# Attention plus gated feed-forward on one core: the first three blocks of chunk 0 spread over the attention rounds, another order of loads, useless matmuls in the first waits

## Chip, cores, metric

One core of one Trainium2 chip. The metric is device time in microseconds (us) of one execution. "Faster" and "slower" in a verdict mean by more than 2%.

## The reference, cut to what matters

```python
# q, k, v: (8 batches, 8 heads, 576 positions, 64), float32
kv  = np.einsum('bhsd,bhse->bhde', k, v)
out = np.einsum('bhsd,bhde->bhse', q, kv)
rms = np.sqrt(np.mean(out * out, axis=-1, keepdims=True) + 1e-06)
x   = out / rms * g_norm                       # heads side by side: (4608, 512)
gate = 1.0 / (1.0 + np.exp(-(x @ w_gate)))     # weights (512, 1536), float64
return (gate * (x @ w_val)) @ w_out            # (1536, 512), float64
```

The weights come as float64, so the kernel converts them from bits on VectorE and ScalarE.

## The kernel before

It works on pairs of heads. A pair goes through these steps; the letters are used throughout:

```python
# K   K'V (12 matmuls) and the q transposes (6)        TensorE
# KVO copy of K'V to SBUF          VectorE  | QO  copy of transposed q   ScalarE
# U   q times K'V (5 matmuls)      TensorE  | SQ  square                 ScalarE
# SUM row sums                     VectorE  | ROOT square root           ScalarE
# NORM reciprocal, scaling         VectorE  | X   transposes (5)         TensorE
# XO  scale by g_norm into xT      ScalarE
```

xT of chunk 0 (512 tokens) is made from pairs 0 to 3 (batch 0). Pairs 4 to 7 (batch 1) are needed for chunk 1. The first layer of chunk 0 has twelve blocks f of 8 matmuls (4 of the gate, 4 of the value, 128x512 each); block f needs weights unit f, converted in five VectorE steps and two ScalarE steps:

```python
def s0():
    ...                                             # m = mantissa bits            VectorE
    vec.tensor_scalar(out=m.bitcast(U32), in0=words(u)[1], scalar1=0x000FFFFF, ...)
    nc.scalar.activation(out=m, in_=m.bitcast(U32), func=AF.Identity, scale=2.0 ** -20, bias=one)
def s1():                                           # p = exponent                 VectorE, ScalarE
    ...
def s2(): ...                                       # low word added               VectorE
def s3(): ...                                       # sign                         VectorE
def s4():
    vec.tensor_tensor(out=m, in0=m, in1=d["p"].bitcast(FP32), op=ALU.mult)
    load_unit(u + NST)
...
for n in range(4):
    load_kv(n)
    load_q(n)
    if n == 0:
        load_unit(0)
```

The start of the kernel is in the order of a list of tokens. `c` is one conversion step, `w1` the load of unit 1, `b013` block 0, value, part 3 of 4:

```python
order = """
    K0 QO0 KVO0 U0 c c SQ0 c SUM0 K1 c ROOT0 NORM0 X0 QO1 KVO1 w1 c U1 XO0 K2 SQ1 SUM1 b000 KVO2
    ROOT1 QO2 NORM1 b010 U2 X1 SQ2 K3 XO1 SUM2 ROOT2 b001 KVO3 QO3 w2 NORM2 U3 X2 SQ3 K4 XO2 SUM3
    ...
    SUM5 ROOT5 b012 KVO6 QO6 NORM5 U6 c X5 SQ6 K7 XO5 SUM6 ROOT6 b003 KVO7 QO7 NORM6 U7 c X6 SQ7
    b013 XO6 SUM7 b100 c ROOT7 b110 G NORM7 b101 E X7 c b111 XO7 c b102 b112 c b103 c b113
"""
```

So each round of attention holds one matmul of block 0; of block 1 three matmuls come ahead of the last X, and the rest of it, with blocks 2, 3 and on, comes after the rounds. Later stages (second layer of chunk 0, chunks 1 to 8) aren't touched.

Of the kernel before, what the change touches and what calls it, by code (L numbers as in the profile page):

```python
# [9 lines left out]
FP32 = mybir.dt.float32  # L10
# [3 lines left out]
AF = mybir.ActivationFunctionType  # L14
ALU = mybir.AluOpType
# [4 lines left out]
def kernel(  # L20
# [11 lines left out]
    nc = tc.nc  # L32

    B, H, S, HD = q.shape
    T, DM = out.shape
    DF = moe_w_gate.shape[1]
    P = 128
# [7 lines left out]
    M = S // NU  # L45
# [4 lines left out]
    NFT = DF // P  # L50
    G = 512
    GH = G // 2
    NG = T // G
    NST = 3
# [12 lines left out]
    NE = 2 * NHP  # L67
# [5 lines left out]
    def load_kv(n):  # L73
        if n >= B * NHP:
            return
        b, h0 = n // NHP, 2 * (n % NHP)
        for name, src in (("k", k), ("v", v)):
            t = (first if n < NE else sb).tile([NP, 2, NJ * HD], FP32, tag=name, name=name, bufs=4 if n < NE else 2)
            nc.sync.dma_start(out=t, in_=src[b, h0:h0 + 2].rearrange("h (p j) d -> p h (j d)", j=NJ))
            pairs[n][name] = t  # L80
# [12 lines left out]
    units = [("gv", f) for f in range(NFT)] + [("wo", f) for f in range(0, NFT, 2)]  # L93
# [4 lines left out]
    def load_unit(u):  # L98
        if u >= len(units):
            return  # L100
        kind, f = units[u]
        staged[u] = st = raw.tile([P, 2, DM], I64, tag="st", name="st", bufs=NST)
        for i in range(2):
            if kind == "gv":
                src = (moe_w_gate, moe_w_val)[i].rearrange("(m p) f -> p m f", p=P)[:, :, P * f:P * f + P]
                nc.sync.dma_start(out=st[:, i].rearrange("p (m f) -> p m f", m=NMT), in_=src)
            else:
                nc.sync.dma_start(out=st[:, i], in_=moe_w_out[P * (f + i):P * (f + i) + P, :])

    def words(u):  # L110
        t = staged[u].rearrange("p i f -> p (i f)").bitcast(U32).rearrange("p (n two) -> p n two", two=2)
        return t[:, :, 0], t[:, :, 1]
# [8 lines left out]
    def convert(u):  # L121
        kind, f = units[u]
        vec = nc.vector
        d = {}

        def s0():

            t = const.tile([P, 2, DM], FP32, name=f"{kind}{f}") if kind == "gv" else w2[:, f:f + 2, :]
            if kind == "gv":
                for i, name in enumerate(("wg", "wv")):  # L130
                    w[name, f] = t[:, i].rearrange("p (m f) -> p m f", m=NMT)
            else:
                for i in range(2):
                    w["wo", f + i] = t[:, i]
            d["m"] = m = t.rearrange("p i f -> p (i f)")
            vec.tensor_scalar(out=m.bitcast(U32), in0=words(u)[1], scalar1=0x000FFFFF, scalar2=None,
                              op0=ALU.bitwise_and)
            nc.scalar.activation(out=m, in_=m.bitcast(U32), func=AF.Identity, scale=2.0 ** -20, bias=one)

        def s1():  # L140


            d["p"] = p = raw.tile([P, UW], U32, tag="cz", name="cz", bufs=2)
            vec.tensor_scalar(out=p, in0=words(u)[1], scalar1=20, scalar2=0x7FF, op0=ALU.logical_shift_right,
                              op1=ALU.bitwise_and)
            nc.scalar.activation(out=p.bitcast(I32), in_=p, func=AF.Relu, scale=2.0 ** 23, bias=exp_off)

        def s2():

            m = d["m"]  # L150
            vec.scalar_tensor_tensor(out=m, in0=words(u)[0], scalar=2.0 ** -52, in1=m, op0=ALU.mult, op1=ALU.add)

        def s3():
            p = d["p"]
            vec.scalar_tensor_tensor(out=p, in0=words(u)[1], scalar=0x80000000, in1=p, op0=ALU.bitwise_and,
                                     op1=ALU.bitwise_or)

        def s4():
            m = d["m"]
            vec.tensor_tensor(out=m, in0=m, in1=d["p"].bitcast(FP32), op=ALU.mult)  # L160
            load_unit(u + NST)

        return [s0, s1, s2, s3, s4]

    STEPS = 5
    converts = deque(step for u in range(len(units)) for step in convert(u))
    made = [0]

    def convert_some(n):
        for _ in range(min(n, len(converts))):  # L170
            converts.popleft()()
            made[0] += 1

    def converted(u):
        convert_some(STEPS * (u + 1) - made[0])

    for n in range(4):
        load_kv(n)
        load_q(n)
        if n == 0:  # L180
            load_unit(0)


    w2 = const.tile([P, NFT, DM], FP32, name="w2")
    ident = const.tile([P, P], FP32, name="ident")
# [138 lines left out]
    def gv_tile(c, f):  # L324
        gv[c, f] = hp.tile([P, G], FP32, tag="gv", name="gv")
        return gv[c, f]

    def sg_tile():
        return sb.tile([P, G], FP32, tag="sg", name="sg", bufs=4)
# [14 lines left out]
    psum_ctx = tc.tile_pool(name="psum0", bufs=1, space=bass.MemoryType.PSUM)  # L344
    psum0 = psum_ctx.__enter__()

    def at_ps(kind):
        return psum_at.tile([P, 2, 512], FP32, tag="at", name="at")
# [15 lines left out]
    def mm_ps():  # L364
        return psum.tile([P, 512], FP32, tag="mm", name="mm", bufs=6)
# [19 lines left out]
    late = deque()  # L385

    def plain(c, f, ps):

        converted(f)
        blk = Plain(c, f, ps)  # L390
        for at in range(2 * NMT):
            blk.mm(*divmod(at, NMT))
            if at in (0, 2) and late:
                late.popleft()()
            if at < STEPS:
                convert_some(1)
        late.extend([blk.gate, blk.end])


    KV, KV_OUT, Q, Q_OUT, U, U_SQUARE, U_SUM, U_ROOT, U_NORM, X, X_OUT = range(11)  # L400
    a = [attention(n, early(n)) for n in range(NE)]

    steps = {"K": (KV, Q), "KVO": (KV_OUT,), "QO": (Q_OUT,), "U": (U,), "SQ": (U_SQUARE,), "SUM": (U_SUM,),
             "ROOT": (U_ROOT,), "NORM": (U_NORM,), "X": (X,), "XO": (X_OUT,)}

    order = """
        K0 QO0 KVO0 U0 c c SQ0 c SUM0 K1 c ROOT0 NORM0 X0 QO1 KVO1 w1 c U1 XO0 K2 SQ1 SUM1 b000 KVO2
        ROOT1 QO2 NORM1 b010 U2 X1 SQ2 K3 XO1 SUM2 ROOT2 b001 KVO3 QO3 w2 NORM2 U3 X2 SQ3 K4 XO2 SUM3
        ROOT3 b011 KVO4 QO4 NORM3 U4 c X3 SQ4 K5 XO3 SUM4 c ROOT4 b002 KVO5 QO5 NORM4 U5 c X4 SQ5 K6 XO4
        SUM5 ROOT5 b012 KVO6 QO6 NORM5 U6 c X5 SQ6 K7 XO5 SUM6 ROOT6 b003 KVO7 QO7 NORM6 U7 c X6 SQ7  # L410
        b013 XO6 SUM7 b100 c ROOT7 b110 G NORM7 b101 E X7 c b111 XO7 c b102 b112 c b103 c b113
    """
    blks = {}

    def block01(f):
        if f not in blks:
            t = psum0.tile([P, 2, 512], FP32, tag="kq", name="two") if f else at_ps(None)
            blks[f] = Plain(0, f, [t[:, i] for i in range(2)])
        return blks[f]

    for token in order.split():
        name = token.rstrip("0123456789")
        n = token[len(name):]
        if name == "b":
            block01(int(n[0])).mm(int(n[1]), int(n[2]))
        elif name == "c":
            convert_some(1)
        elif name == "w":
            load_unit(int(n))
        elif name == "G":  # L430
            blks[0].gate()
        elif name == "E":
            blks[0].end()
        else:
            for step in steps[name]:
                a[int(n)][step]()
            if token == "K7":
                first_ctx.__exit__(None, None, None)
                hp = ctx.enter_context(tc.tile_pool(name="hp", bufs=21))
    late.extend([blks[1].gate, blks[1].end])  # L440
    at0 = at_ps(None)
    plain(0, 2, [at0[:, i] for i in range(2)])
    psum_ctx.__exit__(None, None, None)
    psum = ctx.enter_context(tc.tile_pool(name="psum", bufs=1, space=bass.MemoryType.PSUM))
    for f in range(3, NFT):
        plain(0, f, (mm_ps(), mm_ps()))

    ps = [mm_ps() for _ in range(G // P)]
# [3 lines left out]
                         skip_group_check=True)  # L452

    for f in range(0, NFT - 2, 2):
        converted(NFT + f // 2)
        for at in range(2 * G // P):
            second(at % (G // P), f + at // (G // P))
            if late:
                late.popleft()()
            if at < STEPS:  # L460
                convert_some(1)
    raw_ctx.__exit__(None, None, None)


# [12 lines left out]
    sx, tw, s12, s4 = {}, {}, {}, {}  # L477
# [205 lines left out]
```

## Time and profile before

| | before |
|---|---|
| time, median of 4 runs | 1122.92 us (1121.94 to 1125.1) |
| span of the profiled run | 1120.8 us |
| TensorE busy | 1099.2 us (98%) |
| first matmul of chunk 0 | 23.06 us |
| first matmul of block 3 | 68.64 us |

"Busy" of TensorE counts matmuls with modelled ends, so 98% doesn't say that it can't be faster. Two marks are used below to compare runs, both from TensorE's instructions in order of time: the start of chunk 0's first matmul, and the start of block 3. From block 3 to the end of the span it is 1052.2 us in the trace before. A float32 matmul shows as two records in the profile, its halves, so x4 of block 0 are two matmuls. The lines themselves are in the prediction.

### The profile page before, as it was taken

The page shows a single profiled execution, that of the slowest core. Times are in us where ns is not written, and L with a number is a line of the kernel's source. Part 1 is how long each engine was busy: PE and PEld are TensorE (multiplying, and loading weights), DVE is VectorE, ACT ScalarE, POOL GpSimd, SP SyncE. Part 2 cuts the span into 40 slices and gives each one's busy share as a digit, 9 for nine tenths or more (in the row PEclk, how much of TensorE's full clock was granted, in tenths as well). Part 3 has the DMA queues.
Part 4 walks back from the last instruction along what each step waited for, and adds up shares of the span by engine and source line. Part 5 has one row for each costly group of instructions (what it writes and reads, how often), then busy time and mean ns, then how long its engine had stood idle before and what let it go on. Part 6 is the DMA issues. An engine that isn't in the chain of part 4 may idle for free.

```text
span 1120.8 us, 15097 instructions
## 1 busy us (share of the span) xinstructions
PE 1099.2 (98%) x5760; PEld 912.4 (81%) x5760; DVE 570.6 (51%) x1155; ACT 317.8 (28%) x613; POOL 279.3 (25%) x390
## 2 busy tenths in 40 slices
PE   6899999999999999999999999999999999999998
PEld 5544447888888888888888888888888888888887
DVE  3687776554255516552455326551556146615541
ACT  3643321332133303340333214330333022101110
POOL 0000023432043203330243114320333044404420
PEclk9999999999999999999999999999999999999999
DMA  9944412021202012200302120202100000010001
GB/s 231 264 150 151 150 37 80 22 54 30 72 12 54 11 42 54 53 20 19 73 11 54 30 72 11 54 12 61 41 12 1 20 19 1 1 29 10 1 1 38
DMA packets 71591, 57.60 MB, mean 51 GB/s; under 512 B 40800, under 2 KB 65376, under 8 KB 71520
## 3 DMA queue, kind: packets, MB, share of 16 engines
q1 hardware_dynamic: 71360, 56.64, 19.1%
q8 instruction: 46, 0.75, 0.3%
q14 instruction: 25, 0.20, 0.1%
q10 hardware_dynamic: 160, 0.00, 0.0%
HBM read 47.19 MB, written 9.44 MB: 51 GB/s over the span
## 4 chain that ended last, share of the span: by engine, by line
PE 95%; DVE 2%; ACT 1%; issue 1%; DMA 1%; SPq 0%; ACTq 0%; DVEq 0%
PE mm L510 51%; PE mm L590 26%; PE mm L375 6%; PE mm L451 4%; PE at L246 2%; PE at L217 2%; PE at L231 1%; PE at L272 1%; PE at L375 1%; PE two L246 1%; DMA st<-in_moe_w_val_dram 1%; PE two L217 0%; PE two L375 0%; PE two L272 0%; DVE gv L546 0%
## 5 line engine op out<-in xcount | busy, mean ns | idle before, releaser
L496 POOL TENSOR_TENSOR tw<-gv 128x256 f32<-128x256 f32 x192 | 140.0, 740 | 790.7 <-PE mm L510 628.1
L510 PE MATMUL mm<-xT,tw 128*128 128x256 f32 x768 | 182.4, 380 | 1.0 <-DVE gv L522 1.0
L510 PE MATMUL mm<-sx,tw 128*128 128x256 f32 x768 | 182.4, 380 | 0.0
L510 PE MATMUL mm<-xT,gv 128*128 128x256 f32 x768 | 181.6, 379 | 0.0
L510 PEld LDWEIGHTS mm<-xT,gv 128*128 128x128 f32 x768 | 145.5, 190 | 20.1 <-issue 0.5
L510 PEld LDWEIGHTS mm<-xT,tw 128*128 128x128 f32 x768 | 143.3, 190 | 20.2 <-issue 1.8
L510 PEld LDWEIGHTS mm<-sx,tw 128*128 128x128 f32 x768 | 144.1, 190 | 19.0
L496 POOL TENSOR_TENSOR tw<-gv,tw 128x256 f32<-128x256 f32 x192 | 144.5, 773 | 0.0
L539 ACT ACTIVATE sg<-sg 128x256 f32<-128x256 f32 x96 | 39.9, 417 | 213.1 <-DVE sg L538 213.1
L530 DVE TENSOR_TENSOR gv<-mm,sg 128x256 f32<-128x256 f32 x96 | 40.8, 425 | 99.5 <-PE mm L510 99.5
L510 PE MATMUL mm<-sx,gv 128*128 128x256 f32 x384 | 90.9, 379 | 0.0
L590 PE MATMUL mm<-t2w,gv 128*128 128x256 f32 x384 | 89.0, 379 | 0.0
L590 PE MATMUL mm<-w,gv 128*128 128x256 f32 x384 | 88.3, 379 | 0.0
L590 PE MATMUL mm<-w,s 128*128 128x256 f32 x384 | 88.1, 379 | 0.0
L590 PEld LDWEIGHTS mm<-w,s 128*128 128x128 f32 x384 | 72.9, 190 | 9.9
L590 PEld LDWEIGHTS mm<-t2w,gv 128*128 128x128 f32 x384 | 72.5, 190 | 9.6
L590 PEld LDWEIGHTS mm<-w,gv 128*128 128x128 f32 x384 | 72.4, 190 | 9.6
L510 PEld LDWEIGHTS mm<-sx,gv 128*128 128x128 f32 x384 | 72.1, 190 | 9.4
L517 ACT COPY sg<-mm 128x256 f32<-128x256 f32 x96 | 35.8, 373 | 154.1 <-PE mm L510 154.1
L546 DVE TENSOR_TENSOR gv<-gv,sg 128x512 f32<-128x512 f32 x96 | 78.7, 860 | 0.2
L543 DVE TENSOR_TENSOR gv<-mm,gv 128x256 f32<-128x256 f32 x96 | 40.7, 424 | 47.9 <-PE mm L510 47.5
L526 ACT ACTIVATE sg<-mm 128x256 f32<-128x256 f32 x96 | 36.3, 384 | 100.8 <-PE mm L510 100.8
(94 smaller groups left out, 1130.3 us busy)
## 6 DMA issues: line engine op xcount, KB each, us to landing
k<-in_k_dram SPq DMA_DIRECT2D x32, 288.0 KB, 4.8
v<-in_v_dram SPq DMA_DIRECT2D x32, 288.0 KB, 5.1
q<-in_q_dram SPq DMA_DIRECT2D x64, 144.0 KB, 3.0
st<-in_moe_w_gate_dram SPq DMA_DIRECT2D x12, 512.0 KB, 3.7
st<-in_moe_w_val_dram SPq DMA_DIRECT2D x12, 512.0 KB, 4.9
st<-in_moe_w_out_dram SPq DMA_DIRECT2D x12, 512.0 KB, 4.0
out_dram<-sg SPq DMA_DIRECT2D x24, 192.0 KB, 2.3
out_dram<-sg SPq DMA_DIRECT2D x24, 128.0 KB, 2.3
```

What stands on the lines that cost most here:

```text
L246: nc.tensor.matmul(d["u"][:, i], qT[:, M * i:M * i + MU], kvs[n % 2], start=True, stop=True)
L375: nc.tensor.matmul(self.ps[i], w[("wg", "wv")[i], self.f][:, m, :], xT[self.c][:, m, :], start=(m == 0), stop=(m == NMT - 1), skip_group_c ...
L451: nc.tensor.matmul(ps[t], gv[0, f][:, P * t:P * t + P], w["wo", f], start=(f == 0), stop=(f == NFT - 1), skip_group_check=True)
L496: nc.gpsimd.tensor_tensor(out=tw[f, i], in0=b[in0], in1=b[in1] if isinstance(in1, tuple) else tw[f, in1], op=ALU.subtract)
L510: nc.tensor.matmul(ps, wt[:, m, :], xs[:, m, :], start=(new and m == 0), stop=(m == NK - 1), skip_group_check=True)
L517: nc.scalar.copy(out=d["sg"][:, h2], in_=pa)
L526: nc.scalar.activation(out=d["sg"][:, h1], in_=pa, func=AF.Sigmoid)
L530: tt(out=d["h"][:, h2], in0=pb, in1=d["sg"][:, h2], op=ALU.add)
L539: nc.scalar.activation(out=d["sg"][:, h2], in_=d["sg"][:, h2], func=AF.Sigmoid)
L543: tt(out=d["h"][:, h1], in0=pc, in1=d["h"][:, h1], op=ALU.add)
L546: tt(out=d["h"], in0=d["h"], in1=d["sg"], op=ALU.mult)
L590: nc.tensor.matmul(ps, hs(f), ws[:, f, :], start=(new and f == 0), stop=(f == NF2 - 1), skip_group_check=True)
```

## The change

Intent: TensorE waits in the first 60 us and hardly later, so give it chunk 0's blocks as filling there; load in the order in which data is wanted; keep TensorE busy while it waits, so that it runs fast. Its core:

```diff
-        if n == 0:
+        if n == 1:
             load_unit(0)
...
-    order = """
-        K0 QO0 KVO0 U0 c c SQ0 c SUM0 K1 c ROOT0 ...
+    order = """
+        warm10 KV0 Q0 KVO0 QO0 w1 warm3 U0 SQ0 KV1 SUM0 ROOT0 Q1 KVO1 NORM0 QO1 warm3 U1 SQ1 SUM1 X0 c0.0 c0.1
+        XO0 ROOT1 NORM1 warm5 KV2 Q2 KVO2 a0.0 c0.2 X1 a0.1 c0.3 c0.4 QO2 w2 warm2 U2 SQ2 KV3 Q3 b0.0.0 b0.1.0
+        KVO3 XO1 QO3 w3 U3 SUM2 KV4 Q4 ROOT2 NORM2 SQ3 SUM3 ROOT3 X2 XO2 b0.0.1 b0.1.1 b0.0.2 NORM3 X3 KVO4 QO4
+        U4 c1.0 a1.0 c1.1 a1.1 c1.2 c1.3 b0.1.2 KV5 Q5 KVO5 XO3 b0.0.3 b0.1.3 SQ4 c1.4 w4 SUM4 QO5 U5 CG0 CV0
+        KV6 Q6 b1.0.0 ROOT4 NORM4 X4 b1.1.0 b1.0.1 b1.1.1 SQ5 SUM5 ROOT5 KVO6 QO6 XO4 U6 NORM5 X5 c2.0 c2.1 a2.0
+        c2.2 b1.0.2 KV7 Q7 SQ6 SUM6 a2.1 b1.1.2 ROOT6 c2.3 b1.0.3 XO5 b1.1.3 KVO7 QO7 U7 c2.4 NORM6 CG1 X6 CV1
+        b2.0.0 SQ7 XO6 b2.1.0 b2.0.1 c3.0 SUM7 ROOT7 b2.1.1 c3.1 a3.0 a3.1 NORM7 X7 XO7 c3.2 c3.3 c3.4 b2.0.2
+        b2.1.2 b2.0.3 c4.0 S0 S1 b2.1.3 M0 G2 M1 b3.0.0 b3.1.0 a4.0 E2 c4.1 a4.1 c4.2 c4.3 b3.0.1 b3.1.1 b3.0.2
+        b3.1.2 b3.0.3 b3.1.3 c4.4
     """
...
+        elif name == "CG":                     # gate of the block leaves PSUM as it is
+            copies[f, 0] = sg_tile()
+            nc.scalar.copy(out=copies[f, 0], in_=blks[f].ps[0])
+        elif name == "CV":
+            copies[f, 1] = sg_tile()
+            nc.vector.tensor_copy(out=copies[f, 1], in_=blks[f].ps[1])
+        elif name == "S":                      # sigmoid later, on SBUF
+            nc.scalar.activation(out=copies[f, 0], in_=copies[f, 0], func=AF.Sigmoid)
+        elif name == "M":
+            nc.vector.tensor_tensor(out=gv_tile(0, f), in0=copies[f, 1], in1=copies[f, 0], op=ALU.mult)
+        elif name == "warm":
+            for _ in range(f):
+                nc.tensor.matmul(two0[:, 0, 0:P], ident, ident, start=True, stop=True)
```

Here `c0.2` is step 2 of unit 0 on VectorE, `a0.1` the ScalarE part of a step, `b0.1.3` block 0, value, part 3. K is split in KV and Q. `warm10` is ten useless matmuls: the identity times itself, a result that nobody reads. The blocks of the rounds share one pair of tiles (gate, value) of PSUM, the memory in which matmuls leave their sums; `CG` and `CV` copy a finished block out of it, so that the next can have it.

More of the change, by code (lines that the diff above doesn't have):

```diff
@@ L137, in s0, with a0 @@
                               op0=ALU.bitwise_and)
+        def a0():
+            m = d["m"]
             nc.scalar.activation(out=m, in_=m.bitcast(U32), func=AF.Identity, scale=2.0 ** -20, bias=one)
@@ L145, in s1, with a1 @@
                               op1=ALU.bitwise_and)
+        def a1():
+            p = d["p"]
             nc.scalar.activation(out=p.bitcast(I32), in_=p, func=AF.Relu, scale=2.0 ** 23, bias=exp_off)
@@ L160, in s4, with convert_step @@
             vec.tensor_tensor(out=m, in0=m, in1=d["p"].bitcast(FP32), op=ALU.mult)
-            load_unit(u + NST)
-        return [s0, s1, s2, s3, s4]
-    STEPS = 5
-    converts = deque(step for u in range(len(units)) for step in convert(u))
-    made = [0]
-    def convert_some(n):
-        for _ in range(min(n, len(converts))):
-            converts.popleft()()
-            made[0] += 1
-    def converted(u):
-        convert_some(STEPS * (u + 1) - made[0])
+            if u > 1:
+                load_unit(u + NST)
+        return {"c": [s0, s1, s2, s3, s4], "a": [a0, a1]}
+    conversion = [convert(u) for u in range(len(units))]
+    def convert_step(u, i):
+        if u < len(units) and i < 5:
+            conversion[u]["c"][i]()
+            if i < 2:
+                conversion[u]["a"][i]()
     for n in range(4):
@@ L387, in plain @@
     def plain(c, f, ps):
-        converted(f)
         blk = Plain(c, f, ps)
@@ L394, in plain @@
                 late.popleft()()
-            if at < STEPS:
-                convert_some(1)
+            convert_step(f + 1, at)
         late.extend([blk.gate, blk.end])
@@ L401 @@
     a = [attention(n, early(n)) for n in range(NE)]
-    steps = {"K": (KV, Q), "KVO": (KV_OUT,), "QO": (Q_OUT,), "U": (U,), "SQ": (U_SQUARE,), "SUM": (U_SUM,),
-             "ROOT": (U_ROOT,), "NORM": (U_NORM,), "X": (X,), "XO": (X_OUT,)}
+    steps = {"KV": KV, "KVO": KV_OUT, "Q": Q, "QO": Q_OUT, "U": U, "SQ": U_SQUARE, "SUM": U_SUM, "ROOT": U_ROOT,
+             "NORM": U_NORM, "X": X, "XO": X_OUT}
     order = """
-        K0 QO0 KVO0 U0 c c SQ0 c SUM0 K1 c ROOT0 NORM0 X0 QO1 KVO1 w1 c U1 XO0 K2 SQ1 SUM1 b000 KVO2
-        ROOT1 QO2 NORM1 b010 U2 X1 SQ2 K3 XO1 SUM2 ROOT2 b001 KVO3 QO3 w2 NORM2 U3 X2 SQ3 K4 XO2 SUM3
-        ROOT3 b011 KVO4 QO4 NORM3 U4 c X3 SQ4 K5 XO3 SUM4 c ROOT4 b002 KVO5 QO5 NORM4 U5 c X4 SQ5 K6 XO4
-        SUM5 ROOT5 b012 KVO6 QO6 NORM5 U6 c X5 SQ6 K7 XO5 SUM6 ROOT6 b003 KVO7 QO7 NORM6 U7 c X6 SQ7
-        b013 XO6 SUM7 b100 c ROOT7 b110 G NORM7 b101 E X7 c b111 XO7 c b102 b112 c b103 c b113
@@ L412 @@
-    """
-    blks = {}
-    def block01(f):
-        if f not in blks:
-            t = psum0.tile([P, 2, 512], FP32, tag="kq", name="two") if f else at_ps(None)
-            blks[f] = Plain(0, f, [t[:, i] for i in range(2)])
-        return blks[f]
+        warm10 KV0 Q0 KVO0 QO0 w1 warm3 U0 SQ0 KV1 SUM0 ROOT0 Q1 KVO1 NORM0 QO1 warm3 U1 SQ1 SUM1 X0 c0.0 c0.1
+        XO0 ROOT1 NORM1 warm5 KV2 Q2 KVO2 a0.0 c0.2 X1 a0.1 c0.3 c0.4 QO2 w2 warm2 U2 SQ2 KV3 Q3 b0.0.0 b0.1.0
+        KVO3 XO1 QO3 w3 U3 SUM2 KV4 Q4 ROOT2 NORM2 SQ3 SUM3 ROOT3 X2 XO2 b0.0.1 b0.1.1 b0.0.2 NORM3 X3 KVO4 QO4
@@ L421 @@
+        b3.1.2 b3.0.3 b3.1.3 c4.4
+    """
+    blks, copies = {}, {}
+    two0 = at_ps(None)
     for token in order.split():
-        name = token.rstrip("0123456789")
-        n = token[len(name):]
+        name = token.rstrip("0123456789.")
+        n = [int(i) for i in token[len(name):].split(".")]
+        f = n[0]
         if name == "b":
-            block01(int(n[0])).mm(int(n[1]), int(n[2]))
-        elif name == "c":
-            convert_some(1)
-        elif name == "w":
-            load_unit(int(n))
-        elif name == "G":
-            blks[0].gate()
-        elif name == "E":
-            blks[0].end()
-        else:
-            for step in steps[name]:
-                a[int(n)][step]()
-            if token == "K7":
+            if f not in blks:
+                if f == 3:
+                    psum_ctx.__exit__(None, None, None)
+                    psum = ctx.enter_context(tc.tile_pool(name="psum", bufs=1, space=bass.MemoryType.PSUM))
+                    ps = (mm_ps(), mm_ps())
+                else:
+                    t = at_ps(None) if f else two0
+                    ps = (t[:, 0], t[:, 1])
+                blks[f] = Plain(0, f, ps)
+            blks[f].mm(n[1], n[2])
+        elif name == "CG":
[8 more added lines that the diff above has]
+            nc.vector.tensor_tensor(out=gv_tile(0, f), in0=copies[f, 1], in1=copies[f, 0], op=ALU.mult)
+        elif name == "G":
+            blks[f].gate()
+        elif name == "E":
+            blks[f].end()
+        elif name in ("c", "a"):
+            conversion[f][name][n[1]]()
+        elif name == "w":
+            load_unit(f)
+        elif name == "warm":
+            for _ in range(f):
+                nc.tensor.matmul(two0[:, 0, 0:P], ident, ident, start=True, stop=True)
+        else:
+            a[f][steps[name]]()
+            if token == f"Q{NE - 1}":
@@ L438 @@
                 first_ctx.__exit__(None, None, None)
                 hp = ctx.enter_context(tc.tile_pool(name="hp", bufs=21))
-    late.extend([blks[1].gate, blks[1].end])
-    at0 = at_ps(None)
-    plain(0, 2, [at0[:, i] for i in range(2)])
-    psum_ctx.__exit__(None, None, None)
-    psum = ctx.enter_context(tc.tile_pool(name="psum", bufs=1, space=bass.MemoryType.PSUM))
-    for f in range(3, NFT):
+    late.extend([blks[3].gate, blks[3].end])
+    for f in range(4, NFT):
         plain(0, f, (mm_ps(), mm_ps()))
@@ L454 @@
     for f in range(0, NFT - 2, 2):
-        converted(NFT + f // 2)
         for at in range(2 * G // P):
@@ L459 @@
                 late.popleft()()
-            if at < STEPS:
-                convert_some(1)
+            convert_step(NFT + 1 + f // 2, at)
     raw_ctx.__exit__(None, None, None)
```

## The prediction

> **What bounds the kernel now.** I read the busy table by stretches first, then the list of what TensorE waited for, then TensorE's instructions in order of time, then the other engines and the transfers over the same stretch. The busy table (length, then TensorE, weight loads, VectorE, ScalarE, GpSimd, then granted clock, DMA share, GB/s):
>
> ```profile
> 0.00:20.00 20.00, 9.69 (x79) 8.63 (x80) 7.86 (x17) 6.40 (x10) 0.70 (x6) 1.00 1.01 229
> 20.00:40.00 20.00, 17.39 (x183) 12.98 (x181) 9.73 (x22) 11.73 (x25) 0.00 (x0) 1.00 1.08 267
> 40.00:60.00 20.00, 17.80 (x131) 11.57 (x132) 14.42 (x22) 12.03 (x25) 0.00 (x0) 1.00 0.82 197
> 60.00:80.00 20.00, 19.23 (x46) 8.38 (x45) 17.82 (x21) 8.84 (x10) 0.00 (x0) 1.00 0.49 159
> 80.00:100.00 20.00, 20.00 (x48) 8.77 (x47) 15.58 (x18) 7.96 (x9) 0.00 (x0) 1.00 0.47 156
> 160.00:1121.00 961.00, 955.13 (x5140) 835.46 (x5138) 455.92 (x1006) 248.28 (x514) 276.19 (x382) 1.00 0.12 31
> ```
>
> From 80 us on TensorE is full, and in the last 961 us it idles 5.9 us, most of that the tail. The idle time lies in the first 60 us, where the change works: 15.1 us there. No other engine is full there, but the DMA share is about 1 until 54 us. The list of TensorE's waits in the first 62 us (in total, times, longest):
>
> ```profile
> PE two L217 <- DMA v<-in_v_dram: 7.0, 2, 5.2
> PE two L246 <- ACT qT L236: 3.5, 5, 1.9
> PE two L272 <- DVE sq L263: 3.2, 2, 1.9
> PE two L246 <- DVE kv L223: 1.3, 1, 1.3
> PE at L375 <- ACT sg L380: 0.8, 1, 0.8
> ```
>
> And TensorE in order of time (start, length, what):
>
> ```profile
> 5.17 1.55 PE L217 MATMUL two<-v,k 96*64 96x64 f32 x24 [5.17 <-DMA v<-in_v_dram]
> 6.65 1.22 PE L231 MATMUL two<-ident,q 96*128 96x96 f32 x6
> 9.18 2.45 PE L246 MATMUL two<-kv,qT 128*116 128x128 f32 x10 [1.31 <-DVE kv L223]
> ...
> 18.21 1.19 PE L272 MATMUL two<-ident,sq 115*128 115x115 f32 x5 [1.85 <-DVE sq L263]
> 19.20 2.34 PE L246 MATMUL two<-kv,qT 128*116 128x128 f32 x10
> ...
> 23.06 1.91 PE L375 MATMUL at<-xT,gv 128*128 128x512 f32 x4
> ...
> 49.34 1.35 PE L246 MATMUL two<-kv,qT 128*116 128x128 f32 x10 [0.41 <-ACT qT L236]
> ```
>
> The same ten instructions take 2.45 us at 9 us and 1.35 us at 49 us: TensorE is slow until about 21.5 us. In the middle each attention round (4.65 us, from one U group to the next) holds only one matmul of chunk 0, so TensorE waits 0.41 us for the q copy in most rounds, and 1.85 us where a weight conversion stands ahead of it. Blocks 1, 2 and 3 come after the rounds, all but alone on TensorE.
>
> **What the work alone would take.** Groups back to back and fast, from their distances in the chain that ended last: K'V 0.85, Q transposes 0.66, U 1.09, X transposes 0.49 us: 3.09 a pair, 24.7 us for eight pairs. A matmul of chunk 0 is 0.858 us (the chain has 144 half-matmuls, so 72 matmuls, in 61.80 us), a block of eight 6.87, four blocks 27.5. Together 52.2 us. Block 2 ends in the chain at 68.81 us, so block 3 at 75.7. The first real matmul can't start before v lands at 5.1 us. So 75.7 - 5.2 - 52.2 = 18.3 us are lost; 10.6 are the waits above (without the first 5.2), some 5.4 the slow matmuls, the rest ends of groups. **18 us, 1.6% of the span, is all that the change can win**; 2% would be 22.5.
>
> **What the Trainium skill says.** "TensorE: Matmul & The Clock Gate", Part 1: the array runs at half its clock until about 3.4 us of sustained activity, and falls back after an idle window of that length. The trace agrees in the durations (1.55 against 0.92 us for K'V; busy without a gap from 18.21, fast from about 21.5, 3.3 us later), but its granted clock says 1.00 throughout and doesn't show it. "DMA: Bandwidth & Descriptors", "Issuing engines are not separate DMA queues": transfers share the same 16 engines, so an order of loads moves landings but adds no bandwidth; here 11.3 MB had landed at 47.4 us, some 250 GB/s after the start. "ScalarE: Activation LUTs", "What ACT_TABLE_LOAD costs": some 1.28 us a load; the trace shows 1.28 us at 54.64, between the root of the last pair and the first sigmoid. "Perfetto Trace Analysis", "Optimization Strategy": interleave regimes with different limits; that is what this change does.
>
> **The change part by part.**
>
> *Useless matmuls.* 23 of 128 columns, two halves each. A half is 0.213 us slow and 0.109 fast (ten of U in 2.13 and 1.09 us). The first ten start when the identity is written (1.3 us) and take about 4.3 us, to 5.6: 0.4 us past v's landing, which costs about that; but K'V and Q then run fast, which wins 1.2 us in the first two groups and 1.1 in U0. The other 13 (some 2.8 us) lie in gaps of the chains of pairs 0 to 2.
>
> *Another order of loads.* Unit 0 of the weights now follows pair 1, not pair 0. By bytes, at the times by which before had moved as much: pair 1 by 10.2 us instead of 14.2, unit 0 by 14.2 instead of 11.5, pair 2 by 18, pair 3 by 22 (as before), unit 1 by 29.5, pair 7 by 43, unit 3 by 47.3.
>
> *Where conversions stand.* The changed kernel, built, has the same arithmetic; added are two copies on each of ScalarE and VectorE (about 0.6 us each), by which blocks 0 and 1 leave PSUM with no sigmoid, so that no table load falls among the roots, and the one PSUM pair is free for the next block. Two sigmoids on SBUF follow (1.0 us). One conversion of a unit is 0.6 + 0.6 + 3 x 1.15 = 4.7 us of VectorE and 2.2 of ScalarE.
>
> *The first 24 us*, followed by hand through the new order on all engines with the durations above: K'V0 5.6, q copy to 8.5, U0 to 9.9, its norm to 13.0, U1 12.7 to 14.0, unit 0's first two steps on VectorE 15.6 to 16.8, norm 1 to 18.0, K'V2 from 17.2 (data), unit 0's last three steps 18.6 to 22.1 (before: to 19.7), Q3 at 22.0 (data), first two matmuls of chunk 0 22.7 to 24.4. By then TensorE has done 4 K'V, 4 Q, 3 U, 2 X and 2 matmuls: 6.0 + 3.3 + 1.0 + 1.7 = 12.0 us. Before, these same started at 23.06, so the start itself wins little.
>
> *From 24.4 on* 40.2 us of TensorE work are left to the end of block 3: 64.6 us if it waits no more. Does the rest keep up? VectorE from 22.1 to the end of unit 3's conversion: 5 kv copies 2.3, 6 norms of 1.86 11.2, three units 14.1, two copies 1.3: 28.9 us. In program order, with its waits for ScalarE and for the landings, I get unit 1 at 35.1 (block 1 starts at 38.4), unit 2 at 48.3 (block 2 at 50.5), unit 3 at 57.0 (block 3 at 57.8). ScalarE has about 24 us in that stretch. PSUM: the copies of block 1 end at 50.0, half a us before block 2 wants it. Unit 4 must be converted for 64.7; the table load and sigmoids come first on ScalarE (55.5 to 58.4), and I get 63.2. All close, none late: block 3 ends at 64.7.
>
> *The sum.* 75.7 - 64.7 = 11.0 us. Everything after is the same work, with TensorE full (a block asks 4.7 + 0.7 us of VectorE in 6.9), so nothing gives it back. I take off 1 us, as hand chains leave out handovers and margins are under 1 us in four places: 10.3 us, **1113.0 us**.
>
> **The rivals.** *VectorE becomes the bound.* It is asked 28.9 us in 35, in a strict order where every norm waits for a square and a root. The 1.9 us wait at 40 us before, behind one conversion step, speaks for it. If the margins fail by 2 or 3 us in all, the gain is 7 to 8: 1115 to 1117. *The transfers bound the start.* Pair 2 and pair 3 wait for data in my chain as well, and the DMA share is 1. If the rate there is a tenth lower, everything up to unit 3 lands 2 to 4 us later: gain 7 to 9. For the change: the order puts no weight before it is wanted. *TensorE stays or falls slow.* The gaps between groups up to 17 us may keep the clock down in spite of the useless matmuls; then U0 to U2 and K'V cost about 3 us more on the chain: gain 8, 1115. *The end was hidden anyway*: a later wait (weights, output) eats it: nothing speaks for it, the stretch from 80 us on has full TensorE and half-busy DMA; it would give 1121. *Better than by hand*: first data sooner, or conversion ready at 20 us: 13 to 14, 1109 to 1110.
>
> **Range and chances.** The rivals together lie at 1109 to 1118, which is the range: 1109.0 to 1118.0. More than 2% faster is barred by the 18 us: 0.01. Within 2%: 0.98. Slower by 2%: 0.01, only if the later part is disturbed.
>
> **What would show it right or wrong.** Right: K'V of pair 0 in about 0.9 us at 5.6; the first matmul of chunk 0 at 22 to 23 us; TensorE over 19 us busy of each 20 after 25 us; block 3 done at about 65 us; one table load at about 56 us. Wrong by VectorE: TensorE's waits list shows norm or converted weights (gv) with over 3 us. Wrong by the transfers: K'V or the conversions waiting on DMA after 15 us. Wrong by the clock: U groups of over 2 us after 8 us. And if block 3 is done at 65 but the span is over 1118, the later part has given it back.

## The result

1112.18 us, median of 4 runs (1111.84 to 1112.74), against 1122.92 in the same rounds: ratio 0.9902, 95% interval 0.9885 to 0.9919. A second set of runs, with the experiments, gave 1112.43 against 1123.25, ratio 0.9900 (0.9883 to 0.9916). Clear of noise it is 10.7 us faster. (A ratio is the mean time of one kernel's runs over that of the other's of the same rounds, so not quite the ratio of the medians quoted.) The kernel before scatters more, 1121.7 to 1126.4 over all its runs here; the changed kernel lay between 1111.8 and 1112.8 in all eight of its runs.

The busy table of the changed kernel, same stretches and columns as in the prediction:

```profile
0.00:20.00 20.00, 15.60 (x169) 14.31 (x170) 7.65 (x21) 8.40 (x14) 0.70 (x6) 1.00 1.01 237
20.00:40.00 20.00, 19.95 (x193) 14.26 (x192) 16.26 (x29) 12.02 (x24) 0.00 (x0) 1.00 1.16 268
40.00:60.00 20.00, 20.00 (x100) 11.31 (x99) 17.47 (x25) 15.36 (x28) 0.00 (x0) 1.00 1.11 289
```

TensorE is full from 20 us on; its idle time in the first 60 us fell from 15.1 to 4.5 us. That this fall (10.7 us) is near the gain is chance: 7.5 us of the changed kernel's busy time are the useless matmuls, and some of what was busy before was slow. VectorE, which now converts more weights in this stretch, is busy 33.7 of the 40 us from 20 to 60 us, where it was 24.2. What TensorE still waited for in the first 62 us:

```profile
PE at L458 <- POOL ident masks.py:199: 1.4, 1, 1.4
PE two L235 <- DMA q<-in_q_dram: 1.3, 2, 0.9
PE two L250 <- ACT qT L240: 1.3, 2, 0.7
PE two L276 <- DVE sq L267: 0.5, 1, 0.5
```

All of it comes before 20 us. TensorE in order of time (start, length, what):

```profile
1.36 3.85 PE L458 MATMUL at<-ident 128*128 128x128 f32 x20 [1.36 <-POOL ident masks.py:199]
5.23 0.92 PE L221 MATMUL two<-v,k 96*64 96x64 f32 x24
...
9.04 1.35 PE L250 MATMUL two<-kv,qT 128*116 128x128 f32 x10 [0.58 <-ACT qT L240]
...
13.25 1.35 PE L250 MATMUL two<-kv,qT 128*116 128x128 f32 x10 [0.67 <-ACT qT L240]
...
22.52 1.98 PE L379 MATMUL at<-xT,gv 128*128 128x512 f32 x4
24.34 1.26 PE L250 MATMUL two<-kv,qT 128*116 128x128 f32 x10
...
57.86 17.33 PE L379 MATMUL mm<-xT,gv 128*128 128x512 f32 x40
```

The first K'V takes 0.92 us where it took 1.55, U of pair 0 1.35 where it took 2.45: TensorE is fast from the first real matmul. Chunk 0 still starts at 22.5 us, but block 3 starts at 57.86 instead of 68.64: 10.8 us, all of the gain.

The first mark hides a part of it. When chunk 0 starts, the changed kernel has done four pairs' K'V and q transposes, three U and two X, the kernel before 3, 3, 2 and 1. The same work, with the first two matmuls of chunk 0, is done in the changed kernel when U of pair 3 starts, at 24.34 us, and in the kernel before when its third matmul of chunk 0 starts:

```profile
27.89 1.05 PE L375 MATMUL at<-xT,gv 128*128 128x512 f32 x2
```

So the start wins 3.6 us and the stretch from there to block 3 the other 7.2 (33.5 us against 40.8). Of these, 5.6 us are waits of TensorE in the kernel before that are gone (four of 0.41 us, 1.85, 1.31 and 0.77); the rest isn't attributed.

The second layer of each chunk and what lies between is the same in both traces, down to a wait of 0.7 us of chunk 1 that is in both.

### The profile page after: what moved, and what is told of

The parts are those of the page before. It is cut to its first block, busy times and chain, and to the rows that moved or that the text cites. A ratio compares the mean times of both kernels' runs of the same rounds, so it can differ in the third digit from the quotient of the medians. Undisturbed runs are those within 1.5% of the kernel's fastest.

```text
span 1110.1 us, 15195 instructions
## 1 busy us (share of the span) xinstructions
PE 1099.9 (99%) x5806; PEld 914.9 (82%) x5806; DVE 571.4 (51%) x1157; ACT 319.2 (29%) x615; POOL 279.3 (25%) x390
## 4 chain that ended last, share of the span: by engine, by line
PE 96%; DVE 2%; issue 1%; DMA 0%; ACT 0%; SPq 0%; DVEq 0%; ACTq 0%
PE mm L528 51%; PE mm L608 26%; PE mm L379 6%; PE mm L471 4%; PE at L250 2%; PE at L379 2%; PE at L221 2%; PE at L235 1%; PE at L276 1%; PE two L250 1%; DMA q<-in_q_dram 0%; DVE gv L564 0%; PE two L221 0%; PE two L235 0%; DVE t2w L656 0%
## 5 line engine op out<-in xcount | busy, mean ns | idle before, releaser
L548 DVE TENSOR_TENSOR gv<-mm,sg 128x256 f32<-128x256 f32 x96 | 40.8, 425 | 99.8 <-PE mm L528 99.8
```

The costliest lines, as they stand in the source:

```text
L548: tt(out=d["h"][:, h2], in0=pb, in1=d["sg"][:, h2], op=ALU.add)
```

## The experiments

Two marks of every profiled run (us), and the median time. The median of the kernel before is beside it.

| run | first matmul of chunk 0 | block 3 starts | time | before |
|---|---|---|---|---|
| before | 23.06 | 68.64 | 1122.92 | |
| changed | 22.52 | 57.86 | 1112.18 | 1122.92 |
| changed, again | 23.07 | 58.42 | 1112.43 | 1123.25 |
| e1 no useless matmuls | 28.20 | 65.27 | 1117.88 | 1124.71 |
| e2 unit 0 loaded first | 27.93 | 63.27 | 1116.80 | 1124.71 |
| e3 both undone | 27.92 | 63.18 | 1118.19 | 1124.71 |
| e5 before, with useless matmuls | 23.82 | 69.41 | 1123.38 | 1124.71 |
| e4 blocks 1, 2 behind the rounds | 22.91 | 70.73 | 1125.52 | 1122.43 |
| e6 sign step twice | 23.40 | 60.26 | 1114.54 | 1122.43 |
| e7 sigmoid in the rounds | 22.97 | 60.03 | 1115.14 | 1122.43 |
| e8, e9 attempts at better | 24.81, 22.96 | 61.04, 59.18 | 1115.05, 1113.40 | 1122.43, 1123.25 |
| e10 e2, its wait filled | 26.29 | 61.62 | 1116.26 | 1123.25 |
| e11 e4, its gaps filled | 24.84 | 73.20 | 1125.80 | 1123.25 |

All gave correct results. The calls ran on different chips; the fastest run of the kernel before was 1121.7 to 1122.2 us in each, so losses against the changed kernel (1112.18 and 1112.43) are given across calls. The theory: the gain is chunk 0's work put where TensorE had waited, and it needs a start that is not slower than before. The rival: the gain is the start alone (fast TensorE, data in order), and the blocks only moved along.

**e1: no useless matmuls.**

```diff
-        warm10 KV0 Q0 KVO0 QO0 w1 warm3 U0 ...
+        KV0 Q0 KVO0 QO0 w1 U0 ...            # every warm token taken out
```

> The changed kernel without its 23 useless matmuls. If they keep TensorE fast: K'V0 takes 1.55 us again, U0 and U1 over 2.3, the first matmul of chunk 0 comes 2 to 4 us after 22.5 us, block 3 (57.9 us in the changed kernel) and the end by as much later: 1115 us. If they only cost their own 8 us of TensorE and hide nothing: the first matmul of chunk 0 at 22.5 or earlier, 1112 us or less.

5.5 to 5.7 us lost in time, 7.4 in the profiled run (the slowest of its four, 1119.23). So they hide something, and more than expected. TensorE of e1 in order of time:

```profile
18.08 1.17 PE L276 MATMUL two<-ident,sq 115*128 115x115 f32 x5
...
23.30 2.48 PE L250 MATMUL two<-kv,qT 128*116 128x128 f32 x10
...
28.20 3.67 PE L379 MATMUL at<-xT,gv 128*128 128x512 f32 x4
```

The U groups take 2.48 us, not 1.35, and TensorE is still slow at 28 us, though from 18.08 on it had no wait over 0.4 us. The slow groups from 22.28 us on follow one another without a wait, and unit 0 is converted at 26.15 us: it is the slow TensorE itself that holds chunk 0 back to 28.20.

**e2: unit 0 loaded first, as before.**

```diff
-        if n == 1:
+        if n == 0:
             load_unit(0)
```

> The changed kernel with the weights of unit 0 loaded after pair 0, as before. If the order of loads is a part of the gain: v of pair 1 lands at 13 instead of 9 us, its chain (K'V1, U1, its sum, then the conversion of unit 0 behind it on VectorE) starts some 3 us later, first matmul of chunk 0 at 25.5, 1115 us. If data is early enough either way, or conversion was held by unit 0's landing: no later than 22.5, 1112.

4.4 to 4.6 us lost, 1.5 more than expected. TensorE of e2:

```profile
13.41 0.92 PE L221 MATMUL two<-v,k 96*64 96x64 f32 x24 [3.08 <-DMA v<-in_v_dram]
14.84 1.19 PE L235 MATMUL two<-ident,q 96*128 96x96 f32 x6 [0.51 <-DMA q<-in_q_dram]
...
17.31 2.48 PE L250 MATMUL two<-kv,qT 128*116 128x128 f32 x10
```

Pair 1's data comes 3.1 us late, as expected; but TensorE also falls slow behind that wait, in spite of the useless matmuls around it: K'V of pair 1 still takes 0.92 us, then the q transposes 1.19 instead of 0.69 and U1 2.48. The granted clock is 0.50 from 14.6 to 21.4 us.

**e3: both undone, the order of instructions alone.** (The edits of e1 and e2 together.)

> Both undone, the new order alone. If the two effects lie on the same chain and partly overlap: 4 to 5 us later than the changed kernel, 1116 to 1117, so the order alone still wins 6 us against before. If the start is the whole gain: 1121 or more.

5.8 to 6.0 us lost by the medians: hardly more than by undoing either. The two parts are not two gains to be added: both serve the chain of pairs 0 to 2 ahead of chunk 0, and with either gone TensorE is slow in it (how much of e2's loss that is, e10 tells). And the order alone still wins: block 3 at 63.18 against 68.64, 5.5 us, ratio 0.9952 (0.9932 to 0.9972).

**e5: the kernel before with 19 useless matmuls.**

```diff
-        K0 QO0 KVO0 U0 c c SQ0 c SUM0 K1 c ROOT0 NORM0 X0 QO1 ...
+        warm10 K0 warm3 QO0 KVO0 U0 c c SQ0 c SUM0 K1 warm3 c ROOT0 NORM0 X0 warm3 QO1 ...
```

> The kernel before with 19 useless matmuls (10 ahead of K'V0, 3 after K0, 3 after K1, 3 after X0), all else as before. Its VectorE waits for unit 0's landing at 11.5 us ahead of pair 0's sum, so only what follows X0 gets faster: first matmul of chunk 0 at 21.5 instead of 23.1, time 1.5 us less, 1121. If a fast clock is worth as much here as in the changed kernel: 3 us less or more.

Ratio 1.0001 (0.9977 to 1.0025): no gain seen, where I expected 1.5 us. The interval alone doesn't rule out 1.5; the marks of the trace do for this run, as both come 0.8 us later than in the kernel before. U1 took 2.16 us even so, since TensorE waited 3.4 us for pair 1 ahead of it and fell slow, and the last useless matmuls pushed it to 20.34. Useless matmuls without the other order of loads win nothing here. The old order of tokens with both parts of the new start was not run; that the start alone is not the gain rests on e3 above and e4 below.

**e10: e2 with its wait filled.**

```diff
-        ... U0 SQ0 KV1 SUM0 ...
+        ... U0 SQ0 warm13 KV1 SUM0 ...      # on top of e2
```

> e2 (unit 0 loaded first) with 13 more useless matmuls ahead of pair 1's K'V, which fill the 3 us for which TensorE waits there and after which it was slow until 21.7 us. If e2's loss is mostly the slow clock that the wait brings on: first matmul of chunk 0 at 24 or earlier, 1113. If it is the late data itself: clock stays fast, U1 in 1.35, but first matmul of chunk 0 at 27 (1 us better than e2's 27.9), 1115.5.

```profile
17.02 1.35 PE L250 MATMUL two<-kv,qT 128*116 128x128 f32 x10 [0.58 <-ACT qT L240]
...
26.29 1.99 PE L379 MATMUL at<-xT,gv 128*128 128x512 f32 x4
```

U1 is at 1.35 us again, and the first matmul of chunk 0 comes at 26.29: 1.6 us earlier than in e2, 3.2 to 3.8 later than in the changed kernel's two traces. So of e2's loss some 1.6 us at this mark are the slow clock and the rest is the late data itself, as the second theory said. The time (1116.26) is within e2's scatter; the split rests on the traces.

**e4: blocks 1 and 2 behind the rounds.**

```diff
-        KV6 Q6 b1.0.0 ROOT4 NORM4 X4 b1.1.0 b1.0.1 b1.1.1 SQ5 ...
+        KV6 Q6 ROOT4 NORM4 X4 SQ5 ...        # every b1, b2, CG1, CV1 taken out of the rounds
...
-        c3.4 b2.0.2 b2.1.2 b2.0.3 c4.0 S0 S1 ...
+        c3.4 c4.0 b1.0.0 ... b1.1.3 CG1 CV1 b2.0.0 ... b2.1.3 S0 S1 ...
```

> The changed kernel with blocks 1 and 2 (and the copies of block 1) moved behind the rounds, where they stood before; loads, useless matmuls, conversions and block 0 as in the changed kernel. If spreading the blocks is the larger part of the gain: rounds stay near their length, since VectorE, the data and the chain of a pair hold them (X7 at 49 us at the earliest), the 13.7 us of two blocks come after, block 3 starts 5.5 to 10 us later than 57.9: 1118 to 1122 us. If the start is the gain, the rounds close up as the matmuls leave: at most 3 us later, under 1115.

13 us lost: slower than the kernel before, ratio 1.0027 (1.0013 to 1.0040). The rounds hardly closed up. TensorE of e4:

```profile
41.54 1.35 PE L250 MATMUL two<-kv,qT 128*116 128x128 f32 x10 [2.07 <-DVE gv L136]
...
44.19 0.69 PE L235 MATMUL two<-ident,q 96*128 96x96 f32 x6
47.15 2.48 PE L250 MATMUL two<-kv,qT 128*116 128x128 f32 x10 [2.27 <-ACT qT L240]
...
53.09 0.69 PE L276 MATMUL two<-ident,sq 115*128 115x115 f32 x5 [2.60 <-DVE sq L267]
53.62 8.74 PE L379 MATMUL at<-xT,gv 128*128 128x512 f32 x16
63.76 7.13 PE L379 MATMUL at<-xT,gv 128*128 128x512 f32 x16 [1.40 <-DVE sg L442]
```

The last X group starts at 53.09 us, in the changed kernel at 53.91: with twelve matmuls of 0.86 us taken from ahead of it the rounds are 0.8 us shorter. Their length is set by VectorE and by the chain of a pair, to which a slow U7 (2.48 us) adds 1.1 us here. The moved work comes on top: twelve matmuls, 10.3 us; 1.4 us for block 1's copies (one PSUM pair, so block 2 must wait: a cost of my edit, not of the place); and 1.6 us because the emptied rounds let TensorE fall slow (8.74 us for block 1's sixteen halves, 7.13 for block 2's). So 4.1 of the 12.9 us by which block 3 is late are side effects of this edit, slow clock and copies; the estimate for the place of the twelve matmuls alone is the remaining 8.8 us. Busy table of e4, 40 to 60 us:

```profile
40.00:50.00 10.00, 6.19 (x58) 5.79 (x59) 8.37 (x13) 6.50 (x13) 0.00 (x0) 0.84 1.14 286
50.00:60.00 10.00, 7.40 (x20) 3.47 (x19) 6.47 (x8) 4.76 (x10) 0.00 (x0) 0.82 1.14 256
```

TensorE is busy 6.2 of 10 us while VectorE is busy 8.4, and the granted clock is 0.84. This is the theory's main prop: the filling is worth nearly what it weighs (some 8.8 of 10.3 us), as the rounds take nearly their time with or without it.

**e11: e4 with useless matmuls where the blocks had stood.**

```diff
-        KV6 Q6 ROOT4 NORM4 X4 SQ5 ...
+        KV6 Q6 warm3 ROOT4 NORM4 X4 warm3 warm3 warm3 SQ5 ...   # warm3 for every b1, b2 token in the rounds
```

> e4 (blocks 1 and 2 behind the rounds) with three useless matmuls at each place that a moved one left (0.65 us each, against 0.86). If e4's loss holds a part from the clock that falls in the emptied rounds: U6 in 1.35 instead of 2.48, block 1's 16 halves in 7 instead of 8.7 us, 2 to 3 us less than e4, 1122. The rest of e4's loss, the moved work itself, stays: not under 1120.

A miss in the time: 1125.80, no better than e4. The mechanism showed: U7 (the expectation calls it U6) took 1.25 instead of 2.48 us, block 1's sixteen halves 7.13 instead of 8.74. But the useless matmuls ran past the gaps (2.2 us of them stand between the last X and block 1), and this profiled run, the slowest of its four, began late (chunk 0 at 24.84 us against 22.91, with 2.7 us of waits for q against 0.4, the longest, 1.8 us, followed by a slow stretch). What the clock costs in e4 is therefore only told by the lengths of its groups, not by a time.

**e6: VectorE's margin.** The sign step of units 1 to 3 is done twice, which changes no value.

```diff
-            vec.scalar_tensor_tensor(out=p, ... op0=ALU.bitwise_and, op1=ALU.bitwise_or)
+            for _ in range(2 if u in (1, 2, 3) else 1):
+                vec.scalar_tensor_tensor(out=p, ... op0=ALU.bitwise_and, op1=ALU.bitwise_or)
```

> The changed kernel with the sign step of units 1 to 3 (1.15 us of VectorE, same result when repeated) done twice: 3.5 us more VectorE in the rounds. If its margins are thin (the prediction's view, each under 1 us): norm 6 and the end of unit 3 slip past what TensorE can bridge, block 3 starts 2 us later, 1114. If VectorE's 5 idle us in that stretch take it up: under 0.5 us.

3.5 us more of VectorE cost 2.1 to 2.4 us of time. From the first matmul of chunk 0 to block 3 it is 36.9 us instead of 35.3: 1.5 us in many small waits (U, X6, block 3). The rest lies in the start, ahead of the doubled steps (q of pair 2 was there at 18.51 us), and isn't the edit's. So VectorE is next to being the bound there: 1.5 of 3.5 us of added work go straight into the time.

**e7: sigmoid in the rounds instead of copies.**

```diff
-            nc.scalar.copy(out=copies[f, 0], in_=blks[f].ps[0])
+            nc.scalar.activation(out=copies[f, 0], in_=blks[f].ps[0], func=AF.Sigmoid)
...
-            nc.scalar.activation(out=copies[f, 0], in_=copies[f, 0], func=AF.Sigmoid)     # token S: nothing
```

> The changed kernel with sigmoid done at once where blocks 0 and 1 leave PSUM, in place of copies and later sigmoids. Four more table loads of 1.28 us among the roots. If the copies are needed: roots of pairs 4 and 7 come 2.5 us later, X4 and X7 and unit 3's last steps slip, block 3 1.5 to 2 us later, 1114. If ScalarE has room: no change.

2.7 to 3.0 us lost. ScalarE of e7 (its table loads and what is around them):

```profile
35.76 1.28 ACT L440 ACT_TABLE_LOAD   x1
37.06 0.60 ACT L440 ACTIVATE sg<-at 128x512 f32<-128x512 f32 x1
37.67 1.28 ACT L262 ACT_TABLE_LOAD   x1
...
49.06 1.28 ACT L440 ACT_TABLE_LOAD   x1
...
53.14 1.28 ACT L262 ACT_TABLE_LOAD   x1
```

With one more at 60.73 us that is five loads instead of one after 20 us. X4 and X7 wait 0.7 and 0.6 us for their norm, and block 4 waits 0.7 us for the weights. The two copies of ScalarE pay for themselves.

**e8 and e9: attempts at a better start.**

```diff
-            nc.sync.dma_start(out=t[:, :, e, :], in_=q[...])
+            (nc.sync if n else nc.scalar).dma_start(out=t[:, :, e, :], in_=q[...])       # e8 alone
...
-        ... U1 SQ1 SUM1 X0 c0.0 c0.1 XO0 ROOT1 NORM1 warm5 KV2 Q2 KVO2 a0.0 c0.2 X1 ... warm2 U2 SQ2 KV3 Q3 b0.0.0
+        ... U1 SQ1 c0.0 c0.1 SUM1 X0 XO0 ROOT1 NORM1 a0.0 warm5 KV2 Q2 KVO2 c0.2 X1 ... U2 SQ2 KV3 b0.0.0 XO1 Q3
```

> An attempt at a better one: q of pair 0 issued from ScalarE's queue, the first two steps of unit 0's conversion ahead of pair 1's sum on VectorE, block 0's first matmul ahead of pair 3's q transposes, two useless matmuls fewer. If the chain of pair 0 and 1 with unit 0 sets the start: first matmul of chunk 0 at 20.9 to 21.8 instead of 22.5, block 3 0.5 to 1 us earlier, 1111.5. If data of pairs 3 to 5 sets it: same as the changed kernel.

> The attempt e8 with q of pair 0 back on the sync queue; what is left is the other order of a few tokens and two useless matmuls fewer. If q's queue alone spoilt e8 (q of pair 0 came at 8.9 instead of 7.1 us): first matmul of chunk 0 at 21.3 to 21.8 us, block 3 up to 0.7 us earlier than in the changed kernel, 1111.5. If the new token order is itself no better: 22.5 or later, 1112 to 1113.

Both failed. In e8 TensorE waited for q of pair 0:

```profile
8.91 0.69 PE L235 MATMUL two<-ident,q 96*128 96x96 f32 x6 [1.87 <-DMA q<-in_q_dram]
```

It was issued from 0.74 us on, with the first of all, and was there 1.8 us later than from the sync queue (7.08). k and v of pair 1 were issued at 1.66 and 2.27 us on the sync queue, 1.4 us earlier than in the changed kernel; that they took the share of q is likely, but not shown. Behind this wait of 1.9 us TensorE fell slow as well: U of pair 0 took 2.41 us. e9, without that, starts chunk 0 no earlier (22.96: Q2's data came at 18.07; in the changed kernel it came at 17.43 and, in the second trace, at 18.19, so this varies from run to run) and needs 36.2 us to block 3 where the changed kernel needs 35.3; 0.7 us of that is one group of q transposes (Q3), which its order puts behind the mark. No version better than the changed kernel was found.

## Why the prediction was right

Step by step, by its own marks:

| step | predicted | measured |
|---|---|---|
| first K'V, after the useless matmuls | 5.6 | 5.23, in 0.92 us |
| norm of pair 0 done | 13.0 | 13.57 |
| U1 | 12.7 to 14.0 | 13.25 to 14.60 |
| unit 0 converted | 22.1 | 22.47 |
| first matmul of chunk 0 | 22.7 | 22.52 |
| unit 1, 2, 3 converted | 35.1, 48.3, 57.0 | 35.86, 48.23, 56.89 |
| copies of block 1 end | 50.0 | 50.32 |
| block 2, block 3 start | 50.5, 57.8 | 50.41, 57.86 |
| unit 4 converted (needed at 64.7) | 63.2 | 64.05 |
| time | 1113.0 (1109 to 1118) | 1112.18 |

The bound on the gain (18 us), and with it the chance of only 0.01 for 2%, is borne out: 10.7 us. The engine-by-engine sum held to 0.2 us: block 3 starts 10.8 us earlier, 11.0 were worked out. That it is so close is in part luck: in the six traces with this start (changed twice, e4, e6, e7, e11) chunk 0 starts between 22.52 and 24.84 us, where 22.7 was worked out, and in the second trace of the changed kernel block 3 is 10.2 us earlier. The one term that was off in the sum is the 1 us taken off for handovers: from chunk 0's start on it wasn't there, as the four margins under 1 us held: neither of the changed kernel's traces has a wait of TensorE between 21 and 62 us. The thinnest was 0.1 us (block 1's copies before block 2). e6 shows that they are as thin as was said.

The reason given, chunk 0's work in place of waits, stands: e4 takes it away and loses more than the whole gain (13 us, of which 4.1 are side effects, see there). But two sizes in the rivals were too small, and one sentence misleads. *"TensorE stays or falls slow"* was put at 3 us, for U0 to U2 and K'V; without the useless matmuls it is 5.5 to 5.7, and in the trace of e1 TensorE stays slow to beyond 28 us. *"The transfers bound the start"* was thought of as a lower rate; the rate was no lower (unit 3's landing was expected at 47.3 us by the bytes and its last part came at 45.9), but a pair landing 3 us late costs 4.5 us, because the wait slows TensorE as well (some 1.6 us, by e10). And *"the start itself wins little"* is true of the mark (22.5 against 23.1 us) and misread otherwise: the matmuls of pairs that it counts were not all done at 23.06 in the kernel before. The start wins 3.6 us, as shown above. The new order also needs it more: unit 0's conversion now stands behind pair 1's chain, and chunk 0's first matmul starts 0.05 us after it in the changed kernel and in e2 (converted at 22.47 and 27.88 us), where the kernel before had 3.4 us to spare (19.69). With both parts of the start undone (e3), the same work is done 1.8 us later than in the kernel before, the stretch to block 3 is as much shorter as in the changed kernel (7.2 us), and 5.5 us of the 10.8 stay. Each part alone gives no term for a sum: useless matmuls in the old order won 0; everything but the spreading of blocks 1 and 2 less than 0 in e4 as it ran, an estimated 2 us without e4's side effects.

Left open: why TensorE stayed slow for over 13 us of nearly unbroken work in e1, where before it turned fast after 3.3; what the clock alone costs in e4 as a time (by the lengths of its groups 2.7 us, 1.1 of U7 and 1.6 of block 1); and what the old order would do with the new start.

## What to carry to other kernels

When the bound engine waits in a stage whose length another engine or a dependency chain sets, moving later work of the bound engine into those waits is worth nearly what that work weighs (here an estimated 8.8 of 10.3 us); check first that buffers (here PSUM pairs, freed by a copy without the sigmoid) and the chain's own engine leave room, for VectorE went from 24 to 34 us in 40. Useless matmuls pay only if no long wait is left between them (here waits of 1.8 us in e11, 1.9 in e8, 3.1 in e2 and 3.4 in e5 were followed by slow groups), so order the loads at the same time, and test the parts together and apart. A hand sum over all engines with durations from the trace came within 0.7 us of block 3's start in both traces here; what it could not give is how the parts depend on one another.

## What the Trainium skill lacked or had wrong

- "TensorE: Matmul & The Clock Gate", Part 1, says that TensorE is slow again after an idle window of about 3.4 us. In e4 it was slow at 47.15 us after two idle stretches of 2.1 and 2.3 us, with groups at full speed between them; in e11 a wait of 1.8 us was enough.
- The same part says that about 3.4 us of sustained activity make it fast. That fits the kernel before (3.3 us from 18.21), but in e1 it worked from 18.08 us with no wait over 0.4 us, and the first matmuls of chunk 0 at 28.20 us still took 3.67 us instead of 1.98.
- The same part calls the clock events of a trace unreliable, but no page says that the granted clock misses the slow state before TensorE first turns fast, and only that: it read 1.00 in the first 20 us of the kernel before, whose U group took 2.45 us instead of 1.35, and all through e1; once TensorE had been fast, it read 0.50 wherever groups were slow (0.84 in the mean of e4 from 40 to 50 us, where U7 took 2.48). Added up over windows of half a us, these later slow stretches last 3.4 us in e3, e8 and e11, twice 3.4 in e4, 6.8 in e2 and 10.2 in e5.
- "ScalarE: Activation LUTs", "What ACT_TABLE_LOAD costs", adds a drain of some 1.38 us to every switch of tables. In the changed kernel the scaling ahead of the load ended at 55.65 us, the load took 55.67 to 56.95 and the sigmoid started at 56.97: no such drain is seen.
- "DMA: Bandwidth & Descriptors", "Issuing engines are not separate DMA queues", says that the transfers of all issuing engines interleave and that a second one only saves issue time; it doesn't warn that this can delay the transfer that is needed first. In e8 q, issued 0.9 us earlier from ScalarE's queue, was there 1.8 us later, while the sync queue issued the next pair's k and v 1.4 us earlier (which of the two did it was not tested).
